# Linear attention and two gated layers on one core: moving the attention of later blocks between the four parts of a step's front products, and the store of a split weight piece one step back

## The chip, the cores and the metric

One core of a Trainium2 chip runs the whole computation in one launch. The metric is device time in microseconds (us). The runs of the kernel before took 1833.99, 1834.70 and 1836.22 us; the median is 1834.7 us.

## What is computed

```
q, k, v: (8, 8, 576, 64)      batch, heads, sequence, head width
q_s  = softmax of q over the head width
k_s  = softmax of k over the sequence
attn = q_s @ (k_s^T @ v)                                   per batch and head
x    = attn as (4608, 512)                                 tokens x model width
x    = (sigmoid(x @ w_gate) * (x @ w_val)) @ w_out         inner width 1536
h    = x @ w_in                                            inner width 2048
g    = (a0 + a1 h + a2 h^2 + a3 h^3) / (1 + |b0||h| + |b1| h^2 + 1e-6)
out  = g @ w_out2
```

Each large product is made of three 128x128x512 matmuls, because each operand is split into a high and a low part: high by high, low by high, high by low.

## The kernel before

The 4608 tokens are cut into nine blocks of 512 (`NBLK`). The first gated layer walks over 12 steps of 128 inner columns in each block (`NF1`), and all nine blocks go through it before the second layer starts. Step `i` is `divmod(i, 12)`: block `j`, column `f`. The work of block 0, and the attention of blocks 0 and 1, is ordered by a planner (`in_time`, with the costs in `KINDS`); the change does not touch it. From step 12 on the order is written out by hand, in the loop at L606, and each engine runs its instructions in the order in which the program issues them.

**A step of that loop.** `front_a` is called four times (`kk`), each with six matmuls: three into the PSUM tile `pg` (gate) and three into `pv` (value). This is 24 matmuls on TensorE (PE in the profile). The pool `ps_f` has room for one `pg` and one `pv`, so the next step's first matmul into `pg` waits until ScalarE (ACT) has read it, and the first into `pv` until VectorE (DVE) has. `vec_a` then issues the sigmoid `sg` on ACT (L413), the product `sg` on DVE (L415), the high part `gh` on ACT (L160) and the low part `gl` on DVE (L162). `back_a` issues twelve matmuls into four accumulators `acc` (L430), with the `gh` and `gl` of the step before.

**The attention of blocks 2 to 8** is cut into units of two heads, `u` = 0 to 3, that must be ready at the steps `f` = 4, 6, 8 and 10 of the block before (`UNIT_STEPS`; `d` in the code is that step). For each unit: `km`, the largest k over the sequence per column (DVE, L287); `ps_kt`, a transpose of it on PE (L293), `mx` and a copy on DVE (L296, L298), and `ps_kb`, a transpose back (L303), copied by ACT to `kma` (L306); `k` minus it on POOL (L323), and exp on ACT (L327). For q: the row maximum `qm` (L311), subtraction (L315), exp on ACT (L319), and the division `att_n` (sum `qs`, its inverse, product: L332 to L338) on DVE. Then `ps_kv`, the product of k and v (20 small matmuls, L348), with `rs` (L353, L355) and `kvl` (L364) on DVE and `kvh` (L360) on ACT; `ps_qt`, the transposes of q (L372), with `qh` on ACT (L377) and `ql` on DVE (L379); and `att_d` with two products `ps_xt` that ACT writes to `x_raw` (L398). All these PSUM tiles take turns in the two buffers of the pool `ps_x`.

The work of two neighbouring units falls together: in the odd steps `f` = 3, 5 and 7 stand `ps_kt` and `ps_kb` of unit `u+1` beside `ps_kv` and `ps_qt` of unit `u`. In step 9 only `ps_kv` and `ps_qt` are left, in step 1 only `ps_kt` and `ps_kb`. Blocks 2 to 7 have k and v (24 units), and block 8 only q.

**Where it stands in the step.** There are three lists: `early_work` (`ps_kt` with `mx` and its copy) is issued after the four front parts and the first two instructions of `vec_a`; `work` is issued next, in turns with the rest of `vec_a` and behind the weight preparation; `late_work` (`ps_kb` and the subtraction on POOL) comes after `back_a`. So all attention work of a step is issued after all 24 front matmuls.

**Weight preparation.** The second layer's weights arrive as 64 bit words, and 32 pieces are prepared in the same steps, one in two or three: load (L192), `val` by ACT (L199), four bit operations on DVE (L205 to L218), and the split `hl` on ACT and POOL (L160, L162), which is written to memory (`w2_d`, L230) at the end of the same call. `raw` and `hl` share four buffers. All loads and stores are issued by one queue, that of SyncE (SP), in order.

**Function tables.** sigmoid and exp need different tables on ACT; the compiler puts an `ACT_TABLE_LOAD` ahead of the first instruction that needs another table than the last one did.

Of the kernel before, what the change touches and what calls it, by code (L numbers as in the profile page):

```python
# [20 lines left out]
B, H, S, D = 8, 8, 576, 64  # L21
# [5 lines left out]
NF1, NF2 = F1 // P, F2 // P  # L27
# [91 lines left out]
def kernel(ctx: ExitStack, tc: tile.TileContext, q, k, v, w1, w2, ab_in, out):  # L119


    nc = tc.nc
# [9 lines left out]
    ps_x = ctx.enter_context(tc.tile_pool(name="ps_x", bufs=2, space=PSUM))  # L132
    dram = ctx.enter_context(tc.tile_pool(name="dram", bufs=1, space=DRAM))

    def f32(ap):
        return ap.bitcast(F32)
# [19 lines left out]
    w2_d = [dram.tile([P, 2, NB], F32, name=f"w2_{p}") for p in range(2 * NF2)]  # L156
    x3_d = [dram.tile([KC, P, NB], F32, name=f"x3_{j}") for j in range(NBLK)]

    def split_steps(h, lo, src, lo_eng):
        nc.scalar.activation(h, src, AF.Copy)  # L160
        yield
        lo_eng.tensor_tensor(out=lo, in0=src, in1=f32(h), op=ALU.subtract)  # L162
# [5 lines left out]
    def mm3(ps, wh, wl, xh, xl, first, last):  # L168
        nc.tensor.matmul(ps, wh, xh, start=first, stop=False)  # L169
        nc.tensor.matmul(ps, wl, xh, start=False, stop=False)  # L170
        nc.tensor.matmul(ps, wh, xl, start=False, stop=last)  # L171
# [13 lines left out]
    NW1, NW = 3 * NF1, 3 * NF1 + 2 * NF2  # L185
    raw, val, wt = {}, {}, {}
# [35 lines left out]
    def prep_split(p, eng=nc.gpsimd):  # L222
        if p < NW1:
            wt[p] = [wpool.tile([P, NB], F32R, tag="w", name=n) for n in ("wh", "wl")]
            yield from split_steps(*wt[p], val.pop(p), eng)
        else:
            hl = stage.tile([P, 2, NB], F32R, tag="raw", name="hl")
            yield from split_steps(hl[:, 0], hl[:, 1], val.pop(p), nc.gpsimd)
            yield
            nc.sync.dma_start(out=w2_d[p - NW1], in_=f32(hl))  # L230

    def fetch(p):
        wt[p] = [wpool.tile([P, NB], F32R, tag="w", name=n) for n in ("wh", "wl")]
        for n in range(2):
            nc.sync.dma_start(out=f32(wt[p][n]), in_=w2_d[p - NW1][:, n])

    def prep(stage_of):

        for p, n in stage_of:
            yield from (prep_load, prep_abs, prep_bits_a, prep_bits_b, prep_split)[n](p) or ()  # L240
            yield

    def mix(*jobs):
# [7 lines left out]
    def run(*jobs):  # L251

        jobs = list(jobs)
        while jobs:
            for x in list(jobs):
                if next(x, jobs) is jobs:
                    jobs.remove(x)

    def wa(f, i):
        return wt[at1[f, i]]  # L260
# [144 lines left out]
    def front_a(f, kk, pg, pv):  # L405
        for i, ps in enumerate((pg, pv)):
            wh, wl = wa(f, i)
            s = slice(kk * P, (kk + 1) * P)
            mm3(ps, wh[:, s], wl[:, s], x_h[:, kk, :], x_l[:, kk, :], kk == 0, kk == KC - 1)

    def vec_a(j, f, pg, pv):
        sg = tmp.tile([P, NB], F32, tag="t0", name="sg", bufs=1)
        nc.scalar.activation(sg, pg, AF.Sigmoid)  # L413
        yield
        nc.vector.tensor_tensor(out=sg, in0=pv, in1=sg, op=ALU.mult)  # L415
        yield
        gh = tmp.tile([P, NB], F32R, tag="gh", name="gh")
        gl = tmp.tile([P, NB], F32R, tag="gl", name="gl")
        g_t["a", j, f] = (gh, gl)
        late = nc.gpsimd if j == NBLK - 1 and f < NF1 - 1 else nc.vector  # L420
        yield from split_steps(gh, gl, sg, late if j else Chosen(("g_l", f)))

    def back_a(j, f):
        if f == 0:
            accs["a", j] = [ps_acc.tile([P, NB], F32, tag="acc", name="acc") for _ in range(KC)]
        gh, gl = g_t.pop(("a", j, f))
        wh, wl = wa(f, 2)
        for m, n in order(f == NF1 - 1):
            x, y = ((wh, gh), (wl, gh), (wh, gl))[n]
            nc.tensor.matmul(  # L430
                accs["a", j][m], x[:, m * P:(m + 1) * P], y, start=(f == 0 and n == 0),
                stop=(f == NF1 - 1 and n == 2))
        if f == NF1 - 1:
            for m, acc in enumerate(accs.pop(("a", j))):
                if m % 2:
                    nc.vector.tensor_copy(out=x_raw[:, m, :], in_=acc)  # L436
                else:
                    nc.scalar.activation(x_raw[:, m, :], acc, AF.Copy)
                nc.sync.dma_start(out=x3_d[j][m], in_=x_raw[:, m, :])
# [35 lines left out]
    for i in range(2 * NHP):  # L475
        j, u = divmod(i, NHP)
# [40 lines left out]
    for p in range(NW1):  # L517
        op(("load_w", p), partial(prep_load, p), p >= STAGES and ("w_sign", p - STAGES))
        same = p - 6 if p < NW1 - 2 else p - 1 if p == NW1 - 1 else -1
        op(("w_abs", p), partial(prep_abs, p), ("load_w", p), same >= 0 and ("w_l", same))  # L520
        chain([("w_clip", p), ("w_cut", p)], prep_bits_a(p), ("w_abs", p))
        chain([("w_low", p), ("w_sign", p)], prep_bits_b(p), ("w_cut", p))
        chain([("w_h", p), ("w_l", p)], prep_split(p, Chosen(("w_l", p))), ("w_sign", p), p and ("w_h", p - 1))
# [34 lines left out]
    for o in in_time(ops, chosen):  # L558
        ops[o][0]()

    work, early_work, late_work = {}, {}, {}

    def at(step, fn, *args):
        work.setdefault(max(step, NF1), []).append((fn, args))

    for j in range(2, NBLK):
        for u in range(NHP):
            d = NF1 * (j - 1) + UNIT_STEPS[u]
            if (j, u) != (2, 0):
                at(d - 5, load_k, j, u) if j < B else None  # L570
                at(d - 5, load_q, j, u)
            if j < B:
                at(d - 4, att_km, j, u)
                early_work.setdefault(max(d - 3, NF1 + 1), []).append((att_kt, (j, u, ps_x, "x")))
                late_work.setdefault(max(d - 3, NF1 + 1), []).append((att_kb, (j, u, ps_x, "x")))
                late_work[max(d - 3, NF1 + 1)].append((att_ks, (j, u, nc.gpsimd)))
                at(d - 2, att_ke, j, u)
                at(d - 3, load_v, j, u)
                at(d - 1, att_kv, j, u)
            at(d - 4, att_qm, j, u)  # L580
            at(d - 4, att_qs, j, u, nc.vector)
            at(d - 2, att_qe, j, u)
            at(d - 2, att_n, j, u, nc.vector)
            at(d - 1, att_q, j, u)
            at(d, att_d, j, u)

    def split_x():
        for kk in range(KC):
            split(x_h[:, kk, :], x_l[:, kk, :], x_raw[:, kk, :], nc.vector)

    def sequence(first, calls):
        yield from first
        for fn, args in calls:
            yield from fn(*args) or ()
            yield


    prep_at = {}
    for p in range(NW1, NW):
        at0 = NF1 + 2 + 5 * (p - NW1) // 2  # L600
        for n, step in enumerate((0, 1, 1, 2, 2)):
            prep_at.setdefault(at0 + step, []).append((p, n))

    NA = NBLK * NF1
# [1 line left out]
    for i in range(NF1, NA):  # L606
        j, f = divmod(i, NF1)
        ps = ps_f.tile([P, NB], F32, tag="f", name="pg"), ps_f.tile([P, NB], F32, tag="f", name="pv")
        for kk in range(KC):
            front_a(f, kk, *ps)  # L610
        vec = vec_a(j, f, *ps)
        next(vec)
        next(vec)
        if i == NF1:
            nc.scalar.activation(babs, ab[:, 4:6], AF.Abs)
        if i == NA - 1:
            nc.scalar.preload_act_table_set("natural_log_exp_and_others")
        if f == NF1 - 1:
            split_x()
        run(sequence((), early_work.get(i, [])))  # L620
        run(prep(prep_at.get(i, [])), sequence(vec, work.get(i, [])))
        if pend:
            back_a(*pend.pop(0))
        run(sequence((), late_work.get(i, [])))
        pend.append((j, f))
        if j == NBLK - 1 and f == 4:
            nc.sync.dma_start(out=x_raw, in_=x3_d[0].rearrange("m p c -> p m c"))
        if i == NA - NF1 - 2:
            att_ctx.close()
        if j == NBLK - 1:  # L630
            while len(wt) < NW and order1[len(wt) - NW1][0] < f - 1:
                fetch(len(wt))
# [84 lines left out]
    for i in range(NBS + LAG):  # L717
        while len(wt) < NW and i >= 0 and order1[len(wt) - NW1][0] < NF1 + i - 1:
            fetch(len(wt))
        if i < NBS:  # L720
            j, f = divmod(i, NF2)
# [57 lines left out]
```

## Time and profile before

| | |
|---|---|
| median of 3 runs | 1834.7 us (1833.99 to 1836.22) |
| the profiled execution's own time | 1834.72 us |
| its span, first to last instruction | 1832.9 us |
| TensorE busy | 1772.1 us, 97% of the span |
| VectorE, ScalarE, POOL busy | 1182.3, 1005.6, 363.3 us |

The span falls into three stages: up to about 175 us block 0 with the planner's order, then the 96 hand-ordered steps, and from about 1043 us the second layer. In the profile a matmul of 512 columns is shown as 0.39 us long while the next starts 0.23 us after it: matmuls overlap, and a gap is only marked where the modelled end of one lies before the start of the next. The distance between starts shows more than the marks.

### The profile page before, as it was taken

How to read it: one execution, taken by the hardware profiler on the slowest of the kernel's cores; microseconds unless marked ns; L12 is line 12 of the kernel's file. 1: busy time of each engine (PE TensorE's matmuls, PEld its weight loads, DVE VectorE, ACT ScalarE, POOL GpSimd, SP SyncE). 2: the span in 40 equal slices, each digit the busy share in tenths (PEclk: the TensorE clock that was granted, in tenths of full speed). 3: DMA queues.
4: the chain of work that ended last, by engine and by line, in shares of the span. 5: the costliest groups of instructions: out<-in, count | busy, mean ns of one | idle time of the engine just before them, and what ended most of it. 6: DMA issues, size and time to landing. Idle time of an engine off the chain costs nothing.

```text
span 1832.9 us, 22295 instructions
## 1 busy us (share of the span) xinstructions
PE 1772.1 (97%) x8384; PEld 1452.7 (79%) x8384; DVE 1182.3 (65%) x1925; ACT 1005.6 (55%) x1652; POOL 363.3 (20%) x279
## 2 busy tenths in 40 slices
PE   5988999999999999999999999999999999999999
PEld 3766787787888878778888888888888888888887
DVE  9998545445455454454430288888888888887876
ACT  4556443444435354443331387777676777777765
POOL 3543010101011010110001122222222222222222
PEclk7999999999999999999999999999999999999999
DMA  6442323223132321312226401010000000000000
GB/s 206 146 150 89 115 68 107 69 64 114 62 123 75 110 79 54 123 61 84 78 77 212 160 24 43 5 47 12 35 23 24 24 24 24 23 24 24 1 24 23
DMA packets 53388, 129.54 MB, mean 71 GB/s; under 512 B 5664, under 2 KB 5664, under 8 KB 53280
## 3 DMA queue, kind: packets, MB, share of 16 engines
q1 hardware_dynamic: 53280, 128.12, 21.0%
q8 instruction: 66, 1.08, 0.2%
q14 instruction: 42, 0.34, 0.1%
HBM read 92.44 MB, written 35.65 MB: 70 GB/s over the span
## 4 chain that ended last, share of the span: by engine, by line
PE 56%; DVE 0%; ACT 0%; issue 0%
PE accb L698 21%; PE ph L171 7%; PE ph L170 7%; PE ph L169 7%; PE acc L430 4%; PE pg L169 1%; PE pv L169 1%; PE pg L171 1%; PE pv L171 1%; PE pg L170 1%; PE pv L170 1%; PE ps_qt L372 0%; PE ps_xt L170 0%; PE ps_xt L169 0%; PE ps_xt L171 0%; DVE km L287 0%
## 5 line engine op out<-in xcount | busy, mean ns | idle before, releaser
L415 DVE TENSOR_TENSOR sg<-pv,sg 128x512 f32<-128x512 f32 x108 | 74.4, 689 | 375.7 <-ACT sg L413 208.1
L162 POOL TENSOR_TENSOR glb<-gb,ghb 128x512 fp32r<-128x512 f32 x144 | 187.3, 1301 | 604.1 <-ACT ghb L160 585.4
L413 ACT ACTIVATE sg<-pg 128x512 f32<-128x512 f32 x108 | 64.5, 597 | 388.8 <-PE pg L171 387.0
L666 ACT ACTIVATE h<-ph 128x512 f32<-128x512 f32 x144 | 86.1, 598 | 196.9 <-PE ph L171 196.8
L169 PE MATMUL pg<-x_h,wh 128*128 128x512 f32 x432 | 172.1, 398 | 1.9 <-ACT sg L413 1.9
L169 PE MATMUL pv<-x_h,wh 128*128 128x512 f32 x432 | 169.3, 392 | 2.0 <-DVE sg L415 2.0
L170 PE MATMUL pv<-x_h,wl 128*128 128x512 f32 x432 | 168.9, 391 | 0.3 <-DVE wl L472 0.3
L171 PE MATMUL pv<-x_l,wh 128*128 128x512 f32 x432 | 168.9, 391 | 0.0
L170 PE MATMUL pg<-x_h,wl 128*128 128x512 f32 x432 | 168.8, 391 | 0.0
L171 PE MATMUL pg<-x_l,wh 128*128 128x512 f32 x432 | 168.7, 391 | 0.0
L698 PE MATMUL accb<-wh,ghb 128*128 128x512 f32 x576 | 158.3, 389 | 0.0
L698 PE MATMUL accb<-wl,ghb 128*128 128x512 f32 x576 | 158.3, 389 | 0.0
L698 PE MATMUL accb<-wh,glb 128*128 128x512 f32 x576 | 158.3, 389 | 0.0
L669 DVE SCALAR_TENSOR_TENSOR ah<-h,babs,ah 128x512 f32<-128x512 f32 x144 | 107.9, 750 | 54.5 <-ACT ah L667 54.5
L162 POOL TENSOR_TENSOR hl<-val,hl 128x512 fp32r<-128x512 f32 x32 | 41.3, 1290 | 475.1 <-ACT hl L160 224.3
L430 PE MATMUL acc<-gh,wl 128*128 128x512 f32 x432 | 122.4, 395 | 5.0 <-POOL wl L472 5.0
L430 PE MATMUL acc<-gh,wh 128*128 128x512 f32 x432 | 125.9, 402 | 0.4 <-DVE x_raw L436 0.3
L698 PEld LDWEIGHTS accb<-wl,ghb 128*128 128x128 f32 x576 | 108.1, 188 | 22.5
L698 PEld LDWEIGHTS accb<-wh,glb 128*128 128x128 f32 x576 | 108.1, 188 | 22.4
L698 PEld LDWEIGHTS accb<-wh,ghb 128*128 128x128 f32 x576 | 108.1, 188 | 22.4
L685 DVE SCALAR_TENSOR_TENSOR u<-ah,r 128x512 f32<-128x512 f32 x144 | 99.3, 690 | 39.5 <-ACT r L675 39.5
L169 PE MATMUL ph<-x_h,wh 128*128 128x512 f32 x320 | 124.5, 389 | 0.0
(129 smaller groups left out, 3974.5 us busy)
## 6 DMA issues: line engine op xcount, KB each, us to landing
raw<-in_w SPq DMA_DIRECT2D x68, 512.0 KB, 4.6
w<-hl SPq DMA_DIRECT2D x32, 512.0 KB, 2.9
v<-in_v SPq DMA_DIRECT2D x30, 325.0 KB, 3.3
k<-in_k SPq DMA_DIRECT2D x30, 320.0 KB, 4.1
q<-in_q SPq DMA_DIRECT2D x36, 256.0 KB, 4.2
x<-x_raw SPq DMA_DIRECT2D x36, 256.0 KB, 2.3
x_raw<-x SPq DMA_DIRECT2D x9, 1024.0 KB, 5.4
out<-ob SPq DMA_DIRECT2D x36, 256.0 KB, 2.3
```

Source lines behind the costliest of these rows:

```text
L162: lo_eng.tensor_tensor(out=lo, in0=src, in1=f32(h), op=ALU.subtract)
L169: nc.tensor.matmul(ps, wh, xh, start=first, stop=False)
L170: nc.tensor.matmul(ps, wl, xh, start=False, stop=False)
L171: nc.tensor.matmul(ps, wh, xl, start=False, stop=last)
L413: nc.scalar.activation(sg, pg, AF.Sigmoid)
L415: nc.vector.tensor_tensor(out=sg, in0=pv, in1=sg, op=ALU.mult)
L430: nc.tensor.matmul(accs["a", j][m], x[:, m * P:(m + 1) * P], y, start=(f == 0 and n == 0), stop=(f == NF1 - 1 and n == 2))
L666: nc.scalar.activation(h2, ph, AF.Square)
L669: nc.vector.scalar_tensor_tensor(out=ah, in0=h2, scalar=babs[:, 1:2], in1=ah, op0=ALU.mult, op1=ALU.add)
L685: nc.vector.scalar_tensor_tensor(out=u, in0=ah, scalar=q_one, in1=r, op0=ALU.add, op1=ALU.mult)
L698: nc.tensor.matmul(accs["b", j][t], x[:, t * P:(t + 1) * P], y, start=(f == 0 and n == 0), stop=(f == NF2 - 1 and n == 2))
```

## The change

The three lists become one, `work`, with the key (step, `kk`): what is due there is issued right after front part `kk` of that step. `ps_kt` comes after part 0, `ps_kb` and POOL's subtraction after part 1, `ps_kv`, `ps_qt` and the loads after part 2, and `att_d`, the exp of k and `att_n` after part 0 of the next step. `att_qm` and `att_qs` are issued one step later than before (`d - 3`), and the exp of q one step earlier, in the odd step (`d - 3`), while the exp of k stays in the even one (`d - 2`). `vec_a` is now issued ahead of the preparation in their turns. The store of a split piece becomes a stage of its own, `prep_store`, one step after the split.

```diff
@@ prep_split
             yield from split_steps(hl[:, 0], hl[:, 1], val.pop(p), nc.gpsimd)
-            yield
-            nc.sync.dma_start(out=w2_d[p - NW1], in_=f32(hl))
+            val[p] = hl
+
+    def prep_store(p):
+        nc.sync.dma_start(out=w2_d[p - NW1], in_=f32(val.pop(p)))
@@ prep
-            yield from (prep_load, prep_abs, prep_bits_a, prep_bits_b, prep_split)[n](p) or ()
+            yield from (prep_load, prep_abs, prep_bits_a, prep_bits_b, prep_split, prep_store)[n](p) or ()
@@ lists of work
-    work, early_work, late_work = {}, {}, {}
-
-    def at(step, fn, *args):
-        work.setdefault(max(step, NF1), []).append((fn, args))
+    work = {}
+
+    def at(step, kk, fn, *args):
+        work.setdefault((step, kk) if step >= NF1 else (NF1, 0), []).append((fn, args))
...
-                at(d - 5, load_k, j, u) if j < B else None
-                at(d - 5, load_q, j, u)
+                at(d - 5, 2, load_k, j, u) if j < B else None
+                at(d - 5, 2, load_q, j, u)
             if j < B:
-                at(d - 4, att_km, j, u)
-                early_work.setdefault(max(d - 3, NF1 + 1), []).append((att_kt, (j, u, ps_x, "x")))
-                late_work.setdefault(max(d - 3, NF1 + 1), []).append((att_kb, (j, u, ps_x, "x")))
-                late_work[max(d - 3, NF1 + 1)].append((att_ks, (j, u, nc.gpsimd)))
-                at(d - 2, att_ke, j, u)
-                at(d - 3, load_v, j, u)
-                at(d - 1, att_kv, j, u)
-            at(d - 4, att_qm, j, u)
-            at(d - 4, att_qs, j, u, nc.vector)
-            at(d - 2, att_qe, j, u)
-            at(d - 2, att_n, j, u, nc.vector)
-            at(d - 1, att_q, j, u)
-            at(d, att_d, j, u)
+                at(d - 4, 1, att_km, j, u)
+                at(d - 3, 0, att_kt, j, u, ps_x, "x")
+                at(d - 3, 1, att_kb, j, u, ps_x, "x")
+                at(d - 3, 1, att_ks, j, u, nc.gpsimd)
+                at(d - 3, 2, load_v, j, u)
+                at(d - 2, 0, att_ke, j, u)
+                at(d - 1, 2, att_kv, j, u)
+            at(d - 3, 0, att_qm, j, u)
+            at(d - 3, 0, att_qs, j, u, nc.vector)
+            at(d - 3, 1, att_qe, j, u)
+            at(d - 2, 0, att_n, j, u, nc.vector)
+            at(d - 1, 2, att_q, j, u)
+            at(d, 0, att_d, j, u)
@@ stages of the preparation
-        for n, step in enumerate((0, 1, 1, 2, 2)):
+        for n, step in enumerate((0, 1, 1, 2, 2, 3)):
@@ the loop over steps
         for kk in range(KC):
             front_a(f, kk, *ps)
+            run(sequence((), work.get((i, kk), [])))
...
-        run(sequence((), early_work.get(i, [])))
-        run(prep(prep_at.get(i, [])), sequence(vec, work.get(i, [])))
+        run(vec, prep(prep_at.get(i, [])))
         if pend:
             back_a(*pend.pop(0))
-        run(sequence((), late_work.get(i, [])))
```

In the changed kernel the lines of the attention and of the first layer have numbers higher by two (L293 is L295). The instructions of block 0 keep their order on every engine; the first difference lies at step 12 or later.

**TensorE, step `f` = 5 of block 1.** Before, from the last front matmul of the step to the first of the next:

```order
L171 MATMUL pv<-x_l,wh 128x512
L293 MATMUL ps_kt<-ident,km 128x128
L348 MATMUL ps_kv<-v,k 64x65 x10
L372 MATMUL ps_qt<-ident,q 128x128 x4
L430 MATMUL acc<-gh,wh 128x512 x4
L430 MATMUL acc<-gh,wl 128x512 x4
L430 MATMUL acc<-gl,wh 128x512 x4
L303 MATMUL ps_kb<-ident,km 128x128
L169 MATMUL pg<-x_h,wh 128x512
```

In the change, from the transpose after part 0 to the one after part 1:

```order
L171 MATMUL pv<-x_l,wh 128x512
L295 MATMUL ps_kt<-ident,km 128x128
L169 MATMUL pg<-x_h,wh 128x512
L170 MATMUL pg<-x_h,wl 128x512
L171 MATMUL pg<-x_l,wh 128x512
L169 MATMUL pv<-x_h,wh 128x512
L170 MATMUL pv<-x_h,wl 128x512
L171 MATMUL pv<-x_l,wh 128x512
L305 MATMUL ps_kb<-ident,km 128x128
```

After part 2 of the same step follow `ps_kv` and `ps_qt`, then the six matmuls of part 3 and the twelve of `back_a`. So between `ps_kt` and `ps_kb` there are six front matmuls and nothing else, between `ps_kt` and `ps_kv` twelve, and only the twelve of `back_a` are left between the last front matmul of a step and the first of the next.

**VectorE, the same step.** Before, from the division of q in the even step before to the copy that `ps_kb` needs:

```order
L338 TENSOR_TENSOR q<-q,qs 128x512
L287 TENSOR_REDUCE km<-k 128x128
L311 TENSOR_REDUCE qm<-q 128x8
L315 TENSOR_TENSOR q<-q,qm 128x512
L415 TENSOR_TENSOR sg<-pv,sg 128x512
L296 TENSOR_REDUCE mx<-ps_kt 128x1
L298 COPY km<-mx 128x128
```

In the change, from the product of the even step before to the first work on `ps_kv`:

```order
L417 TENSOR_TENSOR sg<-pv,sg 128x512
L215 SCALAR_TENSOR_TENSOR val<-raw,val 128x512
L162 TENSOR_TENSOR gl<-sg,gh 128x512
L218 SCALAR_TENSOR_TENSOR val<-raw,val 128x512
L298 TENSOR_REDUCE mx<-ps_kt 128x1
L300 COPY km<-mx 128x128
L313 TENSOR_REDUCE qm<-q 128x8
L317 TENSOR_TENSOR q<-q,qm 128x512
L355 TENSOR_SCALAR rs<-ps_kv 128x1
```

`mx` stood behind the division, `km`, `qm`, the subtraction and this step's own product; now it stands behind the last step's product, `gl` and two operations of the preparation, and `qm` and the subtraction come after it.

**ScalarE, the same step, with what each instruction waits for.** Before, from the exps of the even step to `kma`:

```order
L327 ACT_TABLE_LOAD
L327 ACTIVATE k<-k 128x640 [waits Pool_49]
L319 ACTIVATE q<-q 128x512 [waits DMAHW5_49]
L413 ACT_TABLE_LOAD [waits DVE_49]
L413 ACTIVATE sg<-pg 128x512 [waits PE_49]
L199 ACTIVATE val<-raw 128x512 [waits DMAHW3_49,Pool_49]
L160 ACTIVATE gh<-sg 128x512 [waits DVE_49]
```

In the change, from `kma` to the step's sigmoid:

```order
L308 ACTIVATE kma<-ps_kb 128x128 [waits PE_49]
L321 ACT_TABLE_LOAD [waits DMAHW1_49]
L321 ACTIVATE q<-q 128x512 [waits DVE_49]
L362 ACTIVATE kvh_92<-ps_kv,rs 64x64 [waits DVE_49,PE_49]
L362 ACTIVATE kvh_92<-ps_kv,rs 64x64
L379 ACTIVATE qh<-ps_qt 128x512 [waits PE_49]
L415 ACT_TABLE_LOAD [waits PE_49]
L415 ACTIVATE sg<-pg 128x512 [waits Activation_49]
```

The exp of q and the exp of k shared one visit to the exp table in the even step; now each has its own, and the odd step has two table loads as well. There are 48 more table loads in the program. In the odd step `kvh` and `qh` now stand ahead of the sigmoid, and the wait for the finished `pg` stands on the table load before it.

## Rows read from the trace of the kernel before

**Rows 1.** The page's first line.

```profile
span 1832.9 us, 22295 instructions
```

**Rows 2.** Windows, second layer: length, busy us and (instructions) of PE to POOL, clock, DMA.

```profile
1200.00:1400.00 200.00, 200.00 (x884) 165.60 (x883) 162.06 (x234) 143.44 (x234) 48.10 (x37) 1.00 0.06 22
```

**Rows 3.** Waits of PE, 176 to 1060 us: total us, times, longest.

```profile
PE ps_qt L372 <- DVE mx L296: 12.3, 18, 1.1
PE ps_kb L303 <- DVE kvl L364: 3.7, 7, 1.2
```

**Rows 4.** Timeline of PE, step 5 of block 1: start, us, instruction, [marked idle before].

```profile
223.81 0.39 PE L171 MATMUL pv<-x_l,wh 128*128 128x512 f32 x1
...
226.24 0.63 PE L372 MATMUL ps_qt<-ident,q 128*128 128x128 f32 x4 [1.08 <-DVE mx L296]
...
227.63 1.07 PE L430 MATMUL acc<-gh,wl 128*128 128x512 f32 x4
```

**Rows 5.** Timeline of PE, step 3 of block 2.

```profile
315.51 0.39 PE L171 MATMUL pv<-x_l,wh 128*128 128x512 f32 x1
...
318.17 0.63 PE L372 MATMUL ps_qt<-ident,q 128*128 128x128 f32 x4 [1.15 <-DVE mx L296]
...
319.58 1.08 PE L430 MATMUL acc<-gh,wl 128*128 128x512 f32 x4
```

**Rows 6.** Timeline of PE, step 9 of block 1: ps_kv and ps_qt alone.

```profile
263.98 0.39 PE L171 MATMUL pv<-x_l,wh 128*128 128x512 f32 x1
264.30 0.80 PE L348 MATMUL ps_kv<-v,k 128*64 128x65 f32 x20
265.03 0.66 PE L372 MATMUL ps_qt<-ident,q 128*128 128x128 f32 x4
...
266.46 1.08 PE L430 MATMUL acc<-gh,wl 128*128 128x512 f32 x4
```

**Rows 7.** Timeline of PE, step 1 of block 2: ps_kt alone.

```profile
299.13 0.27 PE L293 MATMUL ps_kt<-ident,km 128*128 128x128 f32 x1
...
300.17 1.08 PE L430 MATMUL acc<-gh,wl 128*128 128x512 f32 x4
```

**Rows 8.** Timeline of DVE, steps 4 and 5 of block 1.

```profile
222.68 1.30 DVE L287 TENSOR_REDUCE km<-k 128x128 f32<-128x640 f32 x1
...
225.22 0.68 DVE L415 TENSOR_TENSOR sg<-pv,sg 128x512 f32<-128x512 f32 x1
225.82 0.28 DVE L296 TENSOR_REDUCE mx<-ps_kt 128x1 f32<-128x128 f32 x1
226.13 0.23 DVE L298 COPY km<-mx 128x128 f32<-128x128 f32 x1
...
227.54 0.15 DVE L353 TENSOR_SCALAR rs<-ps_kv 128x1 f32<-128x1 f32 x1
```

**Rows 9.** Timeline of ACT, steps 5 and 6 of block 1.

```profile
227.99 0.63 ACT L360 ACTIVATE kvh<-ps_kv,rs 64x64 fp32r<-64x64 f32 x2 [1.43 <-DVE rs L355]
228.65 0.60 ACT L377 ACTIVATE qh<-ps_qt 128x512 fp32r<-128x512 f32 x1
...
238.37 1.28 ACT L327 ACT_TABLE_LOAD   x1
239.67 0.74 ACT L327 ACTIVATE k<-k 128x640 f32<-128x640 f32 x1
```

**Rows 10.** Groups of ACT, 176 to 1060 us: busy us, mean ns, idle before and releasers.

```profile
L413 ACT ACTIVATE sg<-pg 128x512 f32<-128x512 f32 x96 | 57.4, 598 | 387.0 <-PE pg L171 387.0
L413 ACT ACT_TABLE_LOAD x28 | 35.9, 1283 | 0.5
...
L199 ACT ACTIVATE val<-raw 128x512 f32<-128x512 f32 x32 | 21.5, 670 | 15.4 <-DMA raw<-in_w 15.2
```

**Rows 11.** Waits of the DMA queue, whole span.

```profile
SPq L230 <- POOL hl L162: 527.4, 32, 27.9
```

## The prediction

> **What bounds the kernel now.** I read the windows first, to see in which stage TensorE (PE) has idle time at all. In the second layer it has none: 200 us hold 884 matmuls and no gap [rows 2]. The change leaves that stage alone, so nothing can be won there, and its rate gives the unit for the rest: 200 / 884 = 0.226 us per matmul of 512 columns, 1.36 us for a front part of six, 0.905 us for four and 2.71 us for the twelve of `back_a`. Next I read PE's waits between 176 and 1060 us, the 96 hand-ordered steps. Two lines hold nearly all of it: `ps_qt` waits 18 times for `mx`, 12.3 us, and `ps_kb` 7 times for `kvl`, 3.7 us [rows 3]. PE works in order, so each of these delays all that follows. 18 is the number of odd steps 3, 5 and 7 in the six blocks that have k and v.
>
> Why does `ps_qt` wait for `mx`? It needs the `ps_x` buffer that holds `ps_kt`, and `mx` is what frees it. The timeline of DVE shows why `mx` is late: it stands behind `km` (1.30 us), `qm`, the subtraction and the step's product; it starts at 225.82 [rows 8], 1.78 us after the end of the front matmuls (223.81 + 0.226 = 224.04) [rows 4].
>
> The marks understate the loss. In step 5 of block 1, from the end of the front matmuls (224.04) to the second group of `acc` (227.63) it is 3.59 us; without the four `acc` matmuls 2.69 us [rows 4]. Clean, the same work costs 1.35 us for `ps_kv` and `ps_qt` (266.46 - 263.98 - 0.226 - 0.905) [rows 6] and 0.135 us for `ps_kt` (1.04 - 0.905) [rows 7], in all 1.48. So 1.21 us are lost, of which 1.08 are marked. In step 3 of block 2 it is 2.94 - 1.48 = 1.46 us, with 1.15 marked [rows 5]. The unmarked part is thus 0.12 to 0.30 us per odd step.
>
> **The change, part by part.**
>
> *The wait of `ps_qt`.* In the change twelve front matmuls (2.7 us) stand between `ps_kt` and `ps_kv`, and `mx` is no longer behind `km`, `qm` and the subtraction. For `ps_qt` the buffer is now that of `ps_kb`, which ACT frees when it copies `kma`, a whole front part earlier. The 12.3 us go.
>
> *The wait of `ps_kb` for `kvl`.* It came because `ps_kb` followed `back_a` directly, while `kvl` still held the buffer. Now nothing of unit `u` is in the buffers at that point; the 3.7 us go.
>
> *The unmarked part.* 18 times 0.12 to 0.30 us, 2.2 to 5.4 us. I take 0.2 each, between the two, 3.6 us. The small cost of mixing kinds of matmuls stays as it was: `ps_kt` and `ps_kb` alone cost about 0.135 us each wherever they stand, `ps_kv` with `ps_qt` 1.35. Sum of what goes: 12.3 + 3.7 + 3.6 = 19.6 us.
>
> *New waits, `ps_kb` for the copy of `mx`.* This is the tightest new order: `ps_kb` comes one front part after `ps_kt`, 1.36 + 0.135 = 1.5 us from start to start. `ps_kt` is shown 0.27 us long [rows 7]; I add 0.1 for the signal, an estimate; `mx` and the copy take 0.54 us from the start of the one to the end of the other [rows 8]. So the copy ends 0.9 us after `ps_kt` starts, and 0.6 us are spare, if DVE is free. Ahead of `mx` stand the last step's product, `gl` and at most two operations of the preparation, all of which follow the last sigmoid; by the durations of ACT and DVE they end within the first front part. I expect no wait in most steps.
>
> *New waits, `pg` for the sigmoid.* Before, attention and `back_a` both stood between two steps' front matmuls; now `back_a` alone does. I count from the start of an odd step: three parts and two transposes, 4.35 us, then `ps_kv` (0.73) [rows 6], so that `rs` can start near 5.2. `kvh` starts 0.45 us after `rs` [rows 8, 9] at 5.65, `qh` 0.66 later at 6.3, ending at 6.9; then the table load, 1.28 us, and the sigmoid, 0.60 [rows 10], ending at 8.8; DVE's product, 0.68 [rows 8], ends at 9.5. The next step's first matmul into `pg` is due at 4 x 1.36 + 0.27 + 1.35 + 2.71 = 9.77, the first into `pv` 0.68 later, at 10.45. So 0.9 us are spare for both.
>
> *More table loads.* 48 more at 1.28 us [rows 10], 62 us on ACT, which is idle for 387 us before the sigmoids alone [rows 10]. They cost nothing while the 0.9 us above hold; without that cover each would cost its excess.
>
> *The store one step later.* SP waits 527.4 us for the split that it is to store, 32 times [rows 11], and loads behind that wait come late: ACT waits 15.2 us for `raw` [rows 10]. PE does not wait for any of it, so I cost it at nothing; what hides it is ACT's idle time. If a buffer of `raw` and `hl` came free late, `val` would be late and with it the next `kma`; a store that lands one step (8.1 us) later still has several steps until its buffer is needed.
>
> For new waits I put 1.5 us, an estimate: a few of the 24 units lose some tenths at `ps_kb`. The lower bound is 0; the upper one is the whole of the wait that `ps_kb` would see if `mx` stayed as late as it is (first rival). The sum: 19.6 - 1.5 = 18.1 us. The profiled execution took 1834.7 us (span 1832.9 [rows 1], 1.8 around it), which is also the median of the runs shown. So **1816.6 us**.
>
> **The rivals.**
>
> *A: `mx` is late after all.* Were DVE as far behind `ps_kt` as now, the copy would end at 226.36, 2.3 us after `ps_kt`'s turn [rows 8], and `ps_kb`, due after 1.5, would wait 0.8 us in 18 steps: 14.8 us, leaving a gain of 4.8 us, 1829.9 us. For it: the product, `gl` and the preparation still come first. Against it: `km` (1.30 us [rows 8]) now runs ahead of the even step's product, and `qm` and the subtraction come behind `mx`. Chance 0.10.
>
> *B, slower: the sigmoid of the odd steps is late.* ACT has in a row `kma`, exp table, exp of q, `kvh`, `qh`, sigmoid table, sigmoid, and the second load starts only when `pg` is finished. From 0.9 us of lateness on, PE waits at `pg` in each of the 18 steps; from 0.9 + 19.6 / 18 = 2.0 us on, the change loses. That would be so if a table switch held ACT for twice what its row shows: 2 x 1.28 = 2.56 us late, 18 x (2.56 - 0.9) = 30 us, 1834.7 - 19.6 + 30 = 1845 us. The trace is against it: the load starts at 238.37 and the next activation at 239.67, 1.30 later [rows 9], so nothing but the load is held up. The Trainium skill, page "ScalarE: Activation LUTs", section "What ACT_TABLE_LOAD costs", says otherwise: a switch costs about 1283 ns of load and about 1380 ns of drain, 2.66 us; by that the odd step's sigmoid would be 2.76 us late and the time 1834.7 - 19.6 + 33.5 = 1848.6 us, an estimate from that page; on the load the trace agrees, on the drain it does not. The same page asks in its section on table sets to batch activations by set, which this change undoes for exp of q and k. Chance 0.06, with lateness from any other cause (`rs` late on DVE, `q` late from its subtraction).
>
> *C: no change.* The waits move: with only `back_a` between two steps, `pg` or `pv` wait about 2 us per odd step and take back what `ps_qt` gives. For it: the cover shrinks by 1.5 us per odd step. Against it: the 0.9 us counted above, and that the waits of PE between 176 and 1060 us name neither [rows 3]. 1834.7 us, chance 0.05.
>
> **How the numbers follow.** The forecast has 0.79. Less than 3.7 us (0.2%) cannot be told from no change. A gives a gain just over that, and 0.03 of its 0.10 fall below it. Faster 0.79 + 0.07 = 0.86; within 0.2% 0.05 + 0.03 = 0.08; slower 0.06. The low end is the sum without new waits and with 0.30 us unmarked: 12.3 + 3.7 + 5.4 = 21.4, 1813.3, taken as 1812.5. The high end takes in half of A: 1834.7 - 19.6 + 1.5 + 7.4 = 1824.0, taken as 1825. Left out are the rest of A, B and C, under 0.2.
>
> **What would show it.** In the changed profile: the line `ps_qt` for `mx` gone, PE's waits between 176 and 1060 us under 4 us in all, the first layer ending (first `ph`) some 18 us earlier, the second layer as long as before. ACT's busy time near 1005.6 + 62 = 1067 us. A shows as `ps_kb` waiting for `km` (the copy), B and C as `pg` for `sg` on ACT or `pv` for `sg` on DVE. The prediction is wrong if these lines exceed 5 us, or if the gain comes without the two old lines going.

## The result, and the profile after

The changed kernel took 1814.28 us (median of four runs, 1813.89 to 1814.99) beside 1835.11 us for the kernel before (four runs, 1833.99 to 1836.22): the ratio is 0.9887, with a 95% interval of 0.987 to 0.9904. The forecast was 1816.6 us, in a range of 1812.5 to 1825.

Where the time went is seen best from two rows of each trace: TensorE's first matmul of step 12, where the hand-ordered steps begin, and the first `ph`, where the second layer does. The kernel before:

```profile
174.40 0.50 PE L169 MATMUL pg<-x_h,wh 128*128 128x512 f32 x1 [0.40 <-ACT sg L413]
...
1042.94 0.39 PE L169 MATMUL ph<-x_h,wh 128*128 128x512 f32 x1
```

The change:

```profile
173.63 0.50 PE L169 MATMUL pg<-x_h,wh 128*128 128x512 f32 x1 [0.43 <-ACT sg L415]
...
1022.11 0.39 PE L169 MATMUL ph<-x_h,wh 128*128 128x512 f32 x1
```

The steps took 868.54 us before and 848.48 us now: 20.06 us less. The second layer took 1832.9 - 1042.94 = 789.96 us before and 1812.1 - 1022.11 = 789.99 now. Block 0's stage, which is the same code, ended 0.77 us earlier. Over all runs of this study step 12 began between 172.1 and 176.1 us, so the length of the hand-ordered steps is the sharper measure below; the same program gave 848.48 and 848.45 us in two executions.

TensorE's waits, whole span, change, the longest ones:

```profile
PE ps_kt L295 <- DVE km L289: 7.5, 3, 5.1
PE ps_kb L305 <- DVE km L300: 4.5, 4, 2.6
PE ps_qt L374 <- ACT kvh L362: 3.8, 1, 3.8
PE pg L169 <- ACT sg L415: 3.5, 4, 1.6
```

None of these lies in the hand-ordered steps: between 176 and 1060 us the same question gives no row at all. Before, it named 12.3 and 3.7 us [rows 3] and two short waits that the rows leave out:

```profile
PE acc L430 <- DVE x_raw L436: 0.3, 1, 0.3
PE ps_kt L293 <- DVE km L287: 0.2, 1, 0.2
```

That is 16.5 us in 27 waits, all gone. What is left is block 0's.

The odd step that was read before is step 5 of block 1. In the kernel before, its `ps_kt` started here:

```profile
224.12 0.30 PE L293 MATMUL ps_kt<-ident,km 128*128 128x128 f32 x1
```

The same step in the change, on TensorE (before: [rows 4]):

```profile
218.77 0.27 PE L295 MATMUL ps_kt<-ident,km 128*128 128x128 f32 x1
...
220.27 0.27 PE L305 MATMUL ps_kb<-ident,km 128*128 128x128 f32 x1
...
221.84 0.80 PE L350 MATMUL ps_kv<-v,k 128*64 128x65 f32 x20
222.58 0.66 PE L374 MATMUL ps_qt<-ident,q 128*128 128x128 f32 x4
...
227.21 0.39 PE L169 MATMUL pg<-x_h,wh 128*128 128x512 f32 x1
```

on VectorE [rows 8]:

```profile
219.08 0.29 DVE L298 TENSOR_REDUCE mx<-ps_kt 128x1 f32<-128x128 f32 x1 [1.13 <-PE ps_kt L295]
219.40 0.66 DVE L300 COPY km<-mx 128x128 f32<-128x128 f32 x1
...
226.34 0.69 DVE L417 TENSOR_TENSOR sg<-pv,sg 128x512 f32<-128x512 f32 x1 [1.22 <-ACT sg L415]
```

and on ScalarE [rows 9]:

```profile
223.80 0.60 ACT L379 ACTIVATE qh<-ps_qt 128x512 fp32r<-128x512 f32 x1
224.41 1.28 ACT L415 ACT_TABLE_LOAD   x1
225.71 0.60 ACT L415 ACTIVATE sg<-pg 128x512 f32<-128x512 f32 x1
```

`mx` now waits for TensorE (1.13 us idle), not TensorE for `mx`: it starts 0.31 us after `ps_kt` does, where it was 1.70 us (224.12 to 225.82 [rows 8]). The sigmoid ends at 226.31, and `pg` is written again from 227.21: 0.90 us spare. The product ends at 227.03, and `pv` is due 0.68 us after `pg`, at 227.89: 0.86 us spare.

### The profile page after: what moved, and what is told of

The parts are those of the page before. It is cut to its first block, busy times and chain, and to the rows that moved or that the text cites. A ratio compares the mean times of both kernels' runs of the same rounds, so it can differ in the third digit from the quotient of the medians.

```text
span 1812.1 us, 22283 instructions
## 1 busy us (share of the span) xinstructions
PE 1769.2 (98%) x8384; PEld 1452.8 (80%) x8384; DVE 1193.6 (66%) x1925; ACT 1072.3 (59%) x1700; POOL 368.1 (20%) x279
## 4 chain that ended last, share of the span: by engine, by line
PE 91%; DVE 6%; issue 1%; ACT 1%; DMA 1%; POOL 0%; ACTq 0%; SPq 0%; DVEq 0%
PE accb L703 22%; PE acc L432 15%; PE ph L171 7%; PE ph L170 7%; PE ph L169 7%; PE pg L169 5%; PE pg L171 5%; PE pg L170 5%; PE pv L169 5%; PE pv L171 5%; PE pv L170 5%; DVE early L215 1%; PE ps_qt L374 1%; PE ps_kv L350 1%; DVE early L218 1%
## 5 line engine op out<-in xcount | busy, mean ns | idle before, releaser
L169 PE MATMUL pg<-x_h,wh 128*128 128x512 f32 x432 | 176.6, 409 | 3.5 <-ACT sg L415 3.5
L170 PE MATMUL ph<-x_h,wl 128*128 128x512 f32 x320 | 124.5, 389 | 0.0
L171 PE MATMUL ph<-x_l,wh 128*128 128x512 f32 x320 | 124.5, 389 | 0.0
```

## Experiments

Lengths of the hand-ordered steps, from the same two rows of each run's profiled execution:

| run | steps, us | over the change |
|---|---|---|
| before | 868.54 | 20.1 |
| change, and once more | 848.48, 848.45 | 0 |
| store alone | 867.26 | 18.8 |
| order alone, and once more | 851.44, 852.23 | 3.0, 3.8 |
| q later on VectorE, in the kernel before | 862.58 | 14.1 |
| q earlier on VectorE, in the change | 848.45 | 0.0 |
| ScalarE 0.6, 1.2, 1.9 us later | 849.20, 859.28, 872.45 | 0.7, 10.8, 24.0 |
| one visit to the exp table | 848.48 | 0.0 |
| POOL's low part twice | 848.46 | 0.0 |
| low part on VectorE | 849.59 | 1.1 |

**The store alone.** To the kernel before:

```diff
-            yield
-            nc.sync.dma_start(out=w2_d[p - NW1], in_=f32(hl))
+            val[p] = hl
...
-        for n, step in enumerate((0, 1, 1, 2, 2)):
+        for n, step in enumerate((0, 1, 1, 2, 2, 3)):
```

> The kernel before, with the store of a split piece one step later and nothing else. My theory (TensorE's waits at ps_qt and ps_kb make up the gain, and both come from the order of the attention work): TensorE waits as before, 12.3 and 3.7 us, and the time stays at 1835 within 2 us; only SP's wait for the split falls from 527 us and ACT's 15 us wait for raw goes. Rival (late loads behind the store hold up the attention): the time falls by 5 us or more.

Measured: ratio 0.9992 (0.9982 to 1.0001), no difference that can be told. SP's wait for the split fell to 389.4 us, ScalarE's wait for `raw` to 0.1, and TensorE's waits stayed in the main (13.0 us at `ps_qt`, 2.5 at `ps_kb`). In the old order the store is worth about the 1.3 us by which the steps of this one execution are shorter.

**The order alone.** To the change:

```diff
-        for n, step in enumerate((0, 1, 1, 2, 2, 3)):
+        for n, step in enumerate((0, 1, 1, 2, 2, 2)):
```

> The change with the store left in the step of the split. My theory: the whole gain is here, 1814 to 1816 us, no marked wait of TensorE in the hand-ordered steps. Rival (the store matters together with the new order, since loads are now issued inside the front parts and stand behind a store that waits for POOL): 1818 us or more, with waits of TensorE for data that came late.

Measured: 1817.94 us, ratio 0.9905 (0.9889 to 0.9921); the steps are 3.0 us longer than the change's. So most of the gain is in the order (17.1 of 20.1 us), and the rival has a part of it. TensorE waits twice in the steps, both times at `ps_kb` for the copy, and one of the two waits holds most of what is missing. TensorE, ScalarE and VectorE of this run, around step 1 of block 6:

```profile
725.36 0.30 PE L305 MATMUL ps_kb<-ident,km 128*128 128x128 f32 x1 [2.01 <-DVE km L300]
...
721.98 0.66 ACT L199 ACTIVATE val<-raw 128x512 f32<-128x512 f32 x1 [2.77 <-DMA raw<-in_w]
...
722.67 0.43 DVE L205 TENSOR_SCALAR val<-val 128x512 f32<-128x512 f32 x1 [2.74 <-ACT val L199]
723.13 0.43 DVE L208 TENSOR_SCALAR val<-val 128x512 uint32<-128x512 uint32 x1
723.47 1.28 DVE L438 COPY x_raw<-acc 128x512 f32<-128x512 f32 x2
724.67 0.28 DVE L298 TENSOR_REDUCE mx<-ps_kt 128x1 f32<-128x128 f32 x1
```

Its queue and POOL show where that begins:

```profile
715.41 1.29 POOL L162 TENSOR_TENSOR hl<-val,hl 128x512 fp32r<-128x512 f32 x1 [27.56 <-DVE val L218]
...
716.72 0.33 SPq L232 DMA_DIRECT2D w<-hl  x1
717.18 0.35 SPq L192 DMA_DIRECT2D raw<-in_w  x1
```

The load of `raw` stands behind a store that waits for POOL; `raw` comes 2.8 us late for `val`, two operations of VectorE wait for `val`, and `mx` stands behind them and two copies of `acc`. In the change the load for the same `val` was issued at 691.13, well ahead of that store, and `val` runs at 719.88 without a wait. The other wait, 0.34 us in step 3 of block 3, has another cause; VectorE and POOL there:

```profile
414.92 1.31 DVE L300 COPY km<-mx 128x128 f32<-128x128 f32 x1
...
414.85 1.30 POOL L162 TENSOR_TENSOR hl<-val,hl 128x512 fp32r<-128x512 f32 x1 [13.36 <-issue]
```

The copy starts 0.07 us after POOL's operation, ends 0.08 us after it, and takes 1.31 us where it usually takes 0.23; the runs on POOL below come back to this. I ran the order alone once more beside the change.

> The change with the store left in the step of the split, once more, beside the change itself on the same chip. Theory after the first look (a load of raw waits behind the store in SP's queue, is late, and holds up val, two operations of VectorE and the copy of mx): 2 to 4 us slower than the change, with ps_kb waiting for the copy once by about 2 us. Rival (the first look was noise): equal within 1 us.

> The changed kernel once more, as the measure for the run beside it: 1814 within 1 us, no marked wait of TensorE in the hand-ordered steps.

Measured: 1817.49 us (1815.62 to 1822.08) and 1815.19 us (1812.66 to 1815.39); the steps 852.23 and 848.45 us, with the same 2.0 us wait at `ps_kb` in the first, and no wait in the second. The two spreads nearly touch (the lowest time of the one is 0.2 us above the highest of the other), so on the whole time the size of the 2.3 us is not settled; the steps and the wait repeat. The steps are 0.8 us longer than in the first execution although only 2.0 us are marked. TensorE's granted clock, the share of full speed at which it was let run, shows why:

```profile
728.42 0.30 PE L305 MATMUL ps_kb<-ident,km 128*128 128x128 f32 x1 [1.96 <-DVE km L300]
...
730.30 0.63 PE L169 MATMUL pg<-x_h,wh 128*128 128x512 f32 x1
730.73 0.63 PE L170 MATMUL pg<-x_h,wl 128*128 128x512 f32 x1
```

After the idle 1.96 us the granted clock of 728 to 732 us is 0.69 in the mean, so part of it ran at 1.2 GHz, the lower level, and eight matmuls start about 0.43 us apart instead of 0.23: 1.6 us, unmarked. After the same wait in the first execution the clock stayed at 1.00.

**VectorE's order alone.** To the kernel before:

```diff
-            at(d - 4, att_qm, j, u)
-            at(d - 4, att_qs, j, u, nc.vector)
+            at(d - 3, att_qm, j, u)
+            at(d - 3, att_qs, j, u, nc.vector)
```

> The kernel before, with the row maximum of q and its subtraction issued one step later, so that on VectorE they stand behind mx and its copy; nothing is moved between front parts. My theory (ps_qt waits because mx is late in VectorE's order): mx starts about 1 us earlier and most of the 12.3 us at ps_qt goes; gain 8 to 15 us, with some waits left since the step's own product is still ahead of mx. Rival (the wait comes from issuing all attention matmuls together, whatever VectorE does): ps_qt still waits about 12 us and the time stays within 3 us of before.

Measured: 1829.74 us, ratio 0.9965 (0.995 to 0.998). TensorE's waits of this run, 176 to 1060 us:

```profile
PE ps_kb L303 <- DVE kvl L364: 4.7, 7, 2.4
PE ps_qt L372 <- DVE mx L296: 4.1, 15, 0.3
```

The cause is right for the greater part: with `qm` and the subtraction behind `mx`, two thirds of the wait at `ps_qt` go. Fifteen short waits are left, with the step's own product still ahead of `mx`, as was expected. The size was set too high: the steps are only 6.0 us shorter. `ps_kb` lost 1.0 us more, and behind its longest wait, 2.42 us before 320.89, the granted clock of 320 to 324 us is 0.58 in the mean: matmuls start 0.43 us apart there too, some 1.4 us that no wait shows.

```profile
320.89 0.45 PE L303 MATMUL ps_kb<-ident,km 128*128 128x128 f32 x1 [2.42 <-DVE kvl L364]
```

**The interleaving without VectorE's new order.** To the change:

```diff
-            at(d - 3, 0, att_qm, j, u)
-            at(d - 3, 0, att_qs, j, u, nc.vector)
+            at(d - 4, 1, att_qm, j, u)
+            at(d - 4, 1, att_qs, j, u, nc.vector)
```

> The change with the row maximum of q and its subtraction back in the even step, between km and that step's product. My theory: the twelve front matmuls between ps_kt and ps_kv cover mx in either order, since the product of the even step waits for its sigmoid anyway; the time stays at 1814 within 2 us. Rival (the order on VectorE alone makes the gain): 5 us or more are lost, at ps_kb for the copy behind mx.

Measured: 1814.79 us, ratio 0.9886 (0.9868 to 0.9904), no wait in the steps. In the new order it does not matter in which step the q work is issued. This is not because the front matmuls cover a late `mx`, as was expected: `mx` is not late. It starts 0.30 to 0.32 us after `ps_kt` in all 24 units, as in the change, so the q work, issued inside the even step, is done before. How much lateness of `mx` the twelve front matmuls could cover is not shown by this run.

**How much is spare ahead of the sigmoid.** The copy `qh` made n times more (n = 1, 2, 3), in the change:

```diff
         nc.scalar.activation(qh, tr, AF.Copy)
+        if j > 1:
+            for _ in range(n):
+                nc.scalar.activation(qh, tr, AF.Copy)
```

> The change with the copy qh on ScalarE made once more in each step that has it (blocks 2 to 8), about 0.65 us ahead of the step's sigmoid. My theory (0.9 us are spare between the odd step's sigmoid and the next step's first matmul into pg): no time is lost, 1814 within 2 us. Rival (the sigmoid is already on the path): 18 steps by 0.65, about 12 us more.

> The change with the copy qh made twice more, about 1.3 us ahead of the sigmoid. My theory: 0.4 us over the spare 0.9 in 18 steps, 5 to 10 us more, 1819 to 1824 us, as waits of pg for sg on ScalarE and of pv for sg on VectorE. Rival (the cover is larger than counted): no loss.

> The change with the copy qh made three times more, about 2 us ahead of the sigmoid. My theory: 1.1 us over the spare 0.9 in 18 steps, some 20 us more, 1832 to 1837 us, so that the gain is gone at the lateness named in rival B. Rival (other slack takes it up): under 10 us more.

Measured: 1814.95, 1826.53 and 1839.01 us; ratios 0.9889 (0.9874 to 0.9903), 0.995 (0.9935 to 0.9964) and 1.0025 (1.0016 to 1.0034). TensorE's only waits after 176 us, with two and with three copies more:

```profile
PE pg L169 <- ACT sg L418: 4.7, 18, 0.3
```

```profile
PE pg L169 <- ACT sg L418: 17.5, 22, 0.9
```

Three copies take 1.86 us in a row, so one is 0.62. One fits (0.7 us in all), two do not, and three make the change slower than the kernel before: rival B's mechanism exists. On a straight line between the runs with two and three copies the 20.1 us are lost at 1.7 us, somewhat before the 2.0 that were put. `pv` is never named, since `pg` waits first. The losses are larger than the marks. One of the 22 waits, 0.4 us, ends at 176.14, where step 12 begins, so it is none of the steps' own: they lose 10.8 us for 4.7 marked in 18 waits and 24.0 for 17.1 in 21, which is 0.34 and 0.33 us more per wait. Both padded runs therefore lost more than was expected (1819 to 1824 and 1832 to 1837 us). By the loss, 0.60 us per odd step for 1.24 us of copies, only about 0.64 us were spare, and not the 0.9 that the rows show from the sigmoid's end to `pg`: a late sigmoid costs more than the time by which it is late, since part of each wait is unmarked (below).

**The table loads.** The exp of q put back beside that of k, in the change:

```diff
-            at(d - 3, 1, att_qe, j, u)
+            at(d - 2, 0, att_qe, j, u)
```

> The change with the exp of q back in the even step beside the exp of k, so that both share one visit to the exp table; 48 table loads fewer. My theory: the loads are covered, so ScalarE is busy for some 60 us less and the time stays at 1814 within 2 us. Rival (the loads cost something at the sigmoid): up to 5 us less. If the division of q on VectorE, which now waits for that exp, delays the even step's product, pv waits for it and some us are lost.

Measured: 1815.65 us, ratio 0.9891 (0.9874 to 0.9907); ScalarE is busy for 1007.1 us where the change has 1072.3, and the steps are as long as before the edit. 48 table loads, 65 us of ScalarE with what goes with them, cost nothing. The edit does move work on VectorE: in its tightest unit `mx` starts 0.86 us after `ps_kt`, and only 0.08 us are left ahead of `ps_kb`.

**POOL beside VectorE's copy.** Two edits of the change: POOL computes the low part twice, or VectorE computes it.

```diff
-            yield from split_steps(hl[:, 0], hl[:, 1], val.pop(p), nc.gpsimd)
+            src = val.pop(p)
+            yield from split_steps(hl[:, 0], hl[:, 1], src, nc.gpsimd)
+            nc.gpsimd.tensor_tensor(out=hl[:, 1], in0=src, in1=f32(hl[:, 0]), op=ALU.subtract)
```

```diff
-            yield from split_steps(hl[:, 0], hl[:, 1], val.pop(p), nc.gpsimd)
+            yield from split_steps(hl[:, 0], hl[:, 1], val.pop(p), nc.vector)
```

> The change with POOL's low part of each split piece computed twice, one right behind the other. In the changed kernel VectorE's copy of mx takes 0.23 us in most units and 0.40 to 0.66 us in nine, where POOL's low part of a piece runs beside it. My theory (that copy, and the product that divides q, are held up while POOL works): the copy takes up to 1.3 us longer in those units, TensorE waits at ps_kb for it, up to 1 us each, 3 to 9 us in all, 1817 to 1823 us. Rival (the long copies have another cause): copies as before, no wait, 1814 within 2 us.

> The change with the low part of each split piece on VectorE instead of POOL. My theory: with POOL out of the way nearly all copies of mx take 0.23 us and the division of q 0.69 us; the 32 operations of 0.69 us on VectorE are covered, 1814 within 2 us. Rival (VectorE becomes late by them): waits of TensorE at ps_kb for the copy, or of pv for the product, and 3 us or more.

Measured: 1813.94 us (ratio 0.9885, 0.9871 to 0.9898) and 1816.41 us (0.9898, 0.9885 to 0.9912). With POOL out of the way all copies are short; VectorE's groups, 176 to 1020 us, in the change and then with the low part on VectorE:

```profile
L340 DVE TENSOR_TENSOR q<-q,qs 128x512 f32<-128x512 f32 x28 | 27.2, 971 | 1.0
...
L300 DVE COPY km<-mx 128x128 f32<-128x128 f32 x24 | 8.3, 347 | 0.8
```

```profile
L340 DVE TENSOR_TENSOR q<-q,qs 128x512 f32<-128x512 f32 x28 | 19.4, 692 | 1.0
...
L300 DVE COPY km<-mx 128x128 f32<-128x128 f32 x24 | 5.5, 227 | 0.8
```

The means hide two sizes: in the change nine divisions take about 1.56 us, each with POOL's low part beside it, and 19 take 0.69; the copy is 0.40 to 0.66 us long in ten units that have POOL's low part beside it, and 0.23 in the other 14. In the kernel before all 28 and 24 were short. So it is POOL that holds the copy up. Doubling POOL's work did not make the delay longer, against my expectation; that run, step 5 of block 1:

```profile
220.43 1.29 POOL L162 TENSOR_TENSOR hl<-val,hl 128x512 fp32r<-128x512 f32 x1 [15.08 <-ACT hl L160]
...
221.14 0.66 DVE L302 COPY km<-mx 128x128 f32<-128x128 f32 x1
...
221.80 1.29 POOL L230 TENSOR_TENSOR hl<-val,hl 128x512 fp32r<-128x512 f32 x1
```

The copy ends at 221.80, 0.08 us after POOL's first operation (221.72), and only then POOL's second one starts: the copy gets in between. None of the 24 copies takes more than 0.66 us in that run. The low part on VectorE costs 1.1 us of the steps, with two short waits of `ps_kb` (0.6 us), which is a part of what its rival named.

## Why the prediction was right

- *What bounds the kernel*: shown. The second layer stayed to 0.03 us, and 20.06 of the 20.83 us between the two profiled executions lie in the hand-ordered steps.
- *The waits of `ps_qt` and `ps_kb`*: both lines are gone, 16.0 us. That two thirds of the wait at `ps_qt` came from `mx` behind the q work is shown by the run with VectorE's order alone; for the rest, with the step's own product ahead of `mx`, and for `kvl` in the buffer of `ps_kb`, no run takes the cause alone. That the new places between the front parts are enough, wherever the q work is issued, is shown by the run with the q work put back.
- *The unmarked part*: I took 0.2 us for 18 waits, 3.6 us. The gain of the steps, 20.06, less the marked 16.5 leaves 3.6 us. The sum is met, but not its parts: it spreads over 27 waits, and the two short ones, 0.5 us, were left out of the forecast. Some of that is luck.
- *New waits*: 1.5 us was put for `ps_kb`; none came. Between the profiled executions the change gained 2.7 us more than the forecast: these 1.5, the two short waits' 0.5, and block 0's 0.77 us, which lies within the scatter of that stage and was no part of the sum. The medians differ from the forecast by 2.3. The order alone does have such waits, 2.4 us marked; with the store they went.
- *`ps_kb`'s spare time*: forecast 0.6 us. In a unit without POOL beside it that is what it was (copy from 183.96 for 0.23 us, `ps_kb` at 184.82). In step 5 of block 1 the copy took 0.66 us, ended at 220.06, and `ps_kb` ran at 220.27: 0.2 us were left. The 0.1 us put for the signal to `mx` was 0.04 there (218.77 + 0.27 to 219.08). No wait came of the long copy, by a small margin that the forecast did not know of; in the order alone the same delay reached 1.31 us once and made TensorE wait.
- *The sigmoid's spare time*: forecast 0.9 us for both, and the rows show 0.90 and 0.86. The padded runs put the edge lower, at about 0.64 us by the time lost.
- *Table loads*: forecast 62 us more on ScalarE and no cost; ScalarE rose by 66.7 us, and undoing it won nothing. The Trainium skill's drain of about 1380 ns ("ScalarE: Activation LUTs", "What ACT_TABLE_LOAD costs") does not show here either: load at 224.41, sigmoid at 225.71, 1.30 us later, the load alone.
- *The store*: "I cost it at nothing" fails. It was right for the old order (about 1.3 us), but in the new one the steps lose 3.0 and 3.8 us without it, of which 2.0 marked at `ps_kb` come by the late load. The step that failed is "PE does not wait for any of it": `val` stands ahead of `mx` on two engines, and the new order gives `ps_kb` only one front part to hide that in. As the change has both parts, the total was not touched.

Rival A did not happen with the change, but its wait is what the order alone shows once. Rival C is excluded by the empty table of waits.

## What to carry to other kernels

When the bounding engine runs in order, put a short dependent chain's links apart by a known stretch of its own work, and count that stretch against the chain: here the 1.5 us from `ps_kt` to `ps_kb` were enough for a chain of 0.9 us, and 0.2 us remained where POOL made it 1.3. Count what has become the new cover as well, and find its edge by padding: 0.62 us cost almost nothing, 1.24 us half of the gain, and 1.86 us more than all of it. An edit that costs nothing in the old order can guard the new one, so cost each part of a change in the order that it will run in.

## What the runs showed that was not expected

A copy on VectorE of 0.23 us took up to 0.66 us in the change, and 1.31 us once in the order alone, where POOL's 1.29 us operation ran beside it, and nine divisions of q 1.56 us, not 0.69; with POOL's low part gone, both were short again in all 24 and 28 cases. The Trainium skill, page "SBUF — State Buffer", section "Who interferes with whom", has it: a VectorE instruction in a two-port mode, which a copy can enter, needs a pair of ports that it shares with POOL, and whoever issues first holds the pair for the whole instruction. The traces agree in the times: POOL's operation started 0.07 us ahead of the longest copy, and the copies at 414.92 and 221.14 both end 0.08 us behind POOL's operation.

In the padded runs a marked wait of TensorE at `pg` cost about 0.3 us more than its mark: 0.16 us, because a matmul of 512 columns is shown 0.16 us longer than the distance to the next one (0.39 against 0.23), and about 0.1 us, because the second matmul after a wait starts 0.33 us after the first (173.63 and 173.96 at step 12 of the change). Short waits can stay unmarked for the same reason. It is no fixed price: the 27 waits of the kernel before cost 3.6 us more than their marks, 0.13 us each, and the waits of 1.96 and 2.42 us that were followed by the lower clock cost over 1 us more.

No version in this study beats the change clear of noise: TensorE has no marked wait left in the steps. The marked waits that remain are in block 0's planned part.
